# Sixteen quads and the q projection in TensorE loops, V in halves, y in two column tiles, and resident code in a decode block

## The chip, the cores and the metric

The kernel runs on one core of one Trainium2 chip. A time is the device time of one execution in microseconds (us). "Span" is the part of it that the profile covers, from the first recorded instruction to the last; a time is about 1.7 to 3.5 us longer than its span. That remainder, time minus span, is called **the closing** below. "Granted clock" is the share of TensorE's full clock that the profile lists as granted.

## The reference, cut to what matters

One decoding step for a batch of 2: layer norm of x (2 x 512), q projection, attention of 32 heads over caches of 8192 positions, output projection, residual, a second layer norm and a gated MLP.

```python
q = (layernorm(x) @ wq).reshape(2, 32, 1, 128)
scores = einsum("bhqd,bhkd->bhqk", q, k_cache) * 128 ** -0.5   # k_cache: 2 x 32 x 8192 x 128, bf16
o = einsum("bhqk,bhkd->bhqd", softmax(scores), v_cache)        # v_cache: the same size
h = x + o.reshape(2, 1, 4096) @ wo
n = layernorm(h)
gate, up = n @ W_gate, n @ W_up                                # 512 x 1376 each
out = h + (relu(gate) * up) @ W_down                           # 1376 x 512
```

The caches are 268 of the 281 MB that have to be read, and every byte is used once.

## The kernel before

K and V pass in 16 "quads" (four heads of one batch element: 8.39 MB of K, 8.39 MB of V). There are two K buffers and one V buffer. For each quad VectorE multiplies K by q and halves the row by additions, then a reduction (`sums`) gives the scores; ScalarE takes the exponentials; TensorE does 64 matmuls with V; VectorE picks the useful lanes of their result (`lanes`); and after four quads four "spread" matmuls and a `gather` bring the heads into place.

```python
def products(n, lo, hi):                       # K x q, then halving additions, all on VectorE
    s.op("dve", lambda: dve.tensor_tensor(out=kp, in0=kp, in1=..q.., op=ALU.mult), ...)
    while width > 8:
        s.op("dve", ..add the two halves of kp..)
...
def fn():                                      # TensorE: 15 quads in a loop, the 16th unrolled
    with pe.Fori(0, NGR * B) as g:
        ..four spread rows..
        with pe.Fori(0, NS - ((g + 1) >> 2)):
            pe.wait_ge(s.sem("v_in"), 16).then_inc(s.sem("v_in"), -16)
            pe.wait_ge(s.sem("p_in"), 1).then_inc(s.sem("p_in"), -1)
            pe.wait_ge(s.sem("o_in"), 1).then_inc(s.sem("o_in"), -1)
            v_matmuls(vt, o_ps[0], 0, T).then_inc(s.sem("pe"), 1)
...
for n in range(L):                             # L = 15
    scores(n, ...)                             # products, sums, exps
    if n + 2 < N: load_k(n + 2)
    if n % NS == 1 and n > 1: gather(n // NS - 1)
    if n: lanes(n - 1)
    if n + 1 < L: load_v(n + 1)
```

The last quad is unrolled: V15 goes into K14's buffer in three pieces and wo into the V buffer in four. All bulk loads are issued by SyncE on one queue, in one fixed order. wq comes first, then K0 in two halves, K1, V0 and so on to W_down. x and the last row of x are small loads issued by ScalarE.

At the end of the program each engine's instructions are laid out in blocks: a `head`, a branch round the looping part, a `rest`, a branch hint to `done`, and a spare block of one nop.

The softmax here doesn't subtract the row's maximum and nothing guards it: scores larger than these inputs give would overflow.

## Time and profile before

| | before |
|---|---|
| time, median of 3 (range) | 660.89 us (659.88 to 661.23) |
| span of the profiled run, whose time was 661.17 | 658.0 us |
| busy share: VectorE, ScalarE, TensorE | 94%, 9%, 18% |
| read | 281.06 MB at 427 GB/s |

Two groups of the page, beside what the prediction shows. The columns are line, engine, operation, operands, count, then busy us and mean ns of one, then the idle time just before the group and what ended most of it.

```profile
L383 DVE TENSOR_TENSOR k<-k,qrep 128x32768 bf16<-128x32768 bf16 (+3 forms) x18 | 275.9, 15327 | 3.6 <-DMA k<-in_A_k_cache_dram 3.6
L365 ACT ACTIVATE qrep<-mm 32x512 bf16<-32x512 f32 x12 | 7.1, 588 | 2.4 <-PE mm L352 2.1
```

In the whole execution VectorE waits 3.6 us for K. The timeline of the start and of the end (start, busy us, engine, line, operation, wait in brackets):

```profile
1.53 2.52 ACTq L290 DMA_DIRECT2D osb<-in_A_x_dram  x1
...
10.37 0.29 PE L313 MATMUL st<-ident,osb 2*128 2x2 bf16 x4 [10.37 <-DMA osb<-in_A_x_dram]
...
14.90 3.63 PE L352 MATMUL mm<-v,om 128*64 128x512 bf16 x16 [1.97 <-DMA v<-in_A_wq_dram]
...
21.68 0.33 SPq L283 DMA_DIRECT2D v<-in_A_v_cache_dram  x1
```
```profile
654.73 0.29 DVE L745 CAST sc<-y 128x128 bf16<-128x128 f32 x1 [1.90 <-PE y L674]
655.04 0.64 SPq L748 DMA_DIRECT2D out_dram<-sc  x1
```

### The profile page before, as it was taken

The page shows a single profiled execution, that of the slowest core. Times are in us where ns is not written, and L with a number is a line of the kernel's source. Part 1 is how long each engine was busy: PE and PEld are TensorE (multiplying, and loading weights), DVE is VectorE, ACT ScalarE, POOL GpSimd, SP SyncE. Part 2 cuts the span into 40 slices and gives each one's busy share as a digit, 9 for nine tenths or more (in the row PEclk, how much of TensorE's full clock was granted, in tenths as well). Part 3 has the DMA queues.
Part 4 walks back from the last instruction along what each step waited for, and adds up shares of the span by engine and source line. Part 5 has one row for each costly group of instructions (what it writes and reads, how often), then busy time and mean ns, then how long its engine had stood idle before and what let it go on. Part 6 is the DMA issues. An engine that isn't in the chain of part 4 may idle for free.

```text
span 658.0 us, 3127 instructions
## 1 busy us (share of the span) xinstructions
PE 116.6 (18%) x1240; PEld 47.6 (7%) x1240; DVE 617.8 (94%) x182; ACT 59.5 (9%) x155; POOL 6.5 (1%) x28
## 2 busy tenths in 40 slices
PE   1300301103030110303002030300303030030365
PEld 1100100001010000101001010100101010010122
DVE  1699999999999999999999999999999999999973
ACT  1401001010101001010100101010010101001110
POOL 3000000000000000000000000000000000000000
PEclk9755655756565575655557565565756556575656
DMA  9999999999999999999999999999999999999996
GB/s 377 450 442 430 406 442 446 442 430 406 442 446 442 430 406 442 446 442 430 406 442 446 442 430 406 442 446 442 430 406 442 446 442 430 406 442 446 412 410 267
DMA packets 6763, 281.09 MB, mean 427 GB/s; under 512 B 772, under 2 KB 872, under 8 KB 1640
## 3 DMA queue, kind: packets, MB, share of 16 engines
q1 hardware_dynamic: 6744, 281.06, 99.0%
q8 instruction: 1, 0.02, 0.0%
q14 instruction: 2, 0.02, 0.0%
q10 hardware_dynamic: 16, 0.01, 0.0%
HBM read 281.06 MB, written 0.00 MB: 427 GB/s over the span
## 4 chain that ended last, share of the span: by engine, by line
DVE 80%; DMA 19%; issue 1%; SPq 0%; PE 0%
DVE k L383 37%; DVE k L389 36%; DMA k<-in_A_k_cache_dram 16%; DVE sc L238 5%; DMA k<-in_B_W_down_dram 3%; DVE osb L472 1%; DVE om L468 1%; SPq L548 0%; SPq L560 0%; DVE ou L238 0%; DVE rep L484 0%; SPq L292 0%; PE y L674 0%; DVE sc L745 0%; SPq L821 0%
## 5 line engine op out<-in xcount | busy, mean ns | idle before, releaser
L383 DVE TENSOR_TENSOR k<-k,qrep 128x32768 bf16<-128x32768 bf16 (+3 forms) x18 | 275.9, 15327 | 3.6 <-DMA k<-in_A_k_cache_dram 3.6
L389 DVE TENSOR_TENSOR k<-k 128x4096 bf16<-128x4096 bf16 (+6 forms) x72 | 267.4, 3714 | 2.5
L425 PE MATMUL o<-v,pm 128*32 128x512 bf16 x960 | 86.5, 539 | 461.6 <-PEq L452 461.6
L402 ACT ACTIVATE pm<-sc 32x256 bf16<-32x256 f32 (+2 forms) x68 | 48.2, 709 | 561.6 <-DVE sc L238 560.9
L425 PEld LDWEIGHTS o<-v,pm 128*32 128x32 bf16 x960 | 36.2, 130 | 511.8 <-issue 506.1
L238 DVE TENSOR_REDUCE sc<-k 128x256 f32<-128x2048 bf16 (+2 forms) x17 | 36.7, 2160 | 0.6
L472 DVE TENSOR_REDUCE osb<-om 128x128 f32<-128x512 f32 x16 | 16.5, 1028 | 0.6
L402 ACT ACTIVATION_READ_ACCUMULATOR pm<-sc 32x1 f32 x68 | 15.9, 233 | 0.0
L432 PE MATMUL rep<-osb,spread 128*32 128x128 f32 x40 | 3.9, 420 | 50.0 <-DVE osb L472 47.1
L468 DVE TENSOR_TENSOR om<-o,turn_of 128x512 f32<-128x512 f32 x16 | 10.9, 681 | 1.8 <-PE o L425 1.8
L320 DVE COPY xc<-st 128x8 f32<-128x8 f32 x1 | 0.2, 167 | 10.7 <-PE st L313 10.7
L425 PE MATMUL o<-k,pm 128*32 128x512 bf16 x64 | 7.4, 629 | 7.3 <-ACT pm L402 4.6
L368 DVE CAST qrep<-mm 32x512 bf16<-32x512 f32 x4 | 2.8, 696 | 5.1 <-PE mm L352 5.1
L365 ACT ACTIVATE qrep<-mm 32x512 bf16<-32x512 f32 x12 | 7.1, 588 | 2.4 <-PE mm L352 2.1
L352 PE MATMUL mm<-v,om 128*64 128x512 bf16 x32 | 6.3, 546 | 2.4 <-DMA v<-in_A_wq_dram 2.0
L541 POOL TENSOR_TENSOR zm<-zm,zx 128x1 f32<-128x1 f32 x1 | 0.2, 189 | 619.2 <-ACT pm L402 619.2
L640 DVE STREAM_TRANSPOSE osb<-mm 128x512 f32<-128x512 f32 x1 | 0.7, 717 | 5.1 <-PE mm L624 5.1
L432 PEld LDWEIGHTS rep<-osb,spread 128*32 128x32 f32 x40 | 1.4, 146 | 52.5 <-DVE osb L472 48.7
L624 PE MATMUL mm<-v 128*2 128x512 bf16 x32 | 4.1, 609 | 0.9 <-DMA v<-in_A_wo_dram 0.8
L425 PEld LDWEIGHTS o<-k,pm 128*32 128x32 bf16 x64 | 2.0, 134 | 12.3 <-ACT pm L402 6.0
L352 PEld LDWEIGHTS mm<-v,om 128*64 128x64 bf16 x32 | 2.5, 149 | 5.8 <-DVE pick L238 2.0
L313 PE MATMUL st<-ident,osb 2*128 2x2 bf16 x4 | 0.3, 172 | 10.4 <-DMA osb<-in_A_x_dram 10.4
(86 smaller groups left out, 35.1 us busy)
## 6 DMA issues: line engine op xcount, KB each, us to landing
k<-in_A_k_cache_dram SPq DMA_DIRECT2D x2, 4096.0 KB, 27.7
v<-in_A_wq_dram SPq DMA_DIRECT2D x1, 4096.0 KB, 13.8
k<-in_A_v_cache_dram SPq DMA_DIRECT2D x1, 4096.0 KB, 31.4
k<-in_A_v_cache_dram SPq DMA_DIRECT2D x1, 3072.0 KB, 38.3
v<-in_A_wo_dram SPq DMA_DIRECT2D x1, 2048.0 KB, 17.6
k<-in_B_W_gate_dram SPq DMA_DIRECT2D x1, 1376.0 KB, 14.7
k<-in_B_W_up_dram SPq DMA_DIRECT2D x1, 1032.0 KB, 16.8
k<-in_A_v_cache_dram SPq DMA_DIRECT2D x1, 1024.0 KB, 40.3
```

The costliest lines, as they stand in the source:

```text
L238: s.op("dve", lambda: dve.tensor_reduce(out=out_, in_=in_, axis=axis, op=ALU.add), reads=reads, writes=writes)
L352: last = pe.matmul(out=ps[h * B * Q:(h + 1) * B * Q], lhsT=xnb[:, c].rearrange("p b q -> p (b q)"), rhs=wq_h[:, c, g:g + QP, h0 + h, :], s ...
L365: s.op("act", lambda src=src, dst=dst: act.activation(out=dst, in_=src, func=ACT.Copy), reads=[f"mm{t}"], writes=[key])
L368: s.op("dve", lambda src=src, dst=dst: dve.tensor_copy(dst, src), reads=[f"mm{t}"], writes=[key])
L383: s.op("dve", lambda: dve.tensor_tensor(out=kp, in0=kp, in1=_view(qrep[:, b, i, :], 0, [[0, hi - lo], [1, Dh]]), op=ALU.mult), reads=keys ...
L389: s.op("dve", lambda half=half, width=width: dve.tensor_tensor(out=kp[:, :, 0:half], in0=kp[:, :, 0:half], in1=kp[:, :, half:width], op=AL ...
L402: last = act.activation(out=p_of[ps, lo // TG:hi // TG, :, h], in_=sc2[n % 2][ps, lo:hi].rearrange("p (g t) -> p g t", t=TG), func=ACT.Exp ...
L425: last = pe.matmul(out=o[g:g + W2], lhsT=pm[:, t // TG, :], rhs=vs[:, t:t + TG, :].rearrange("p t d -> p (t d)"), start=(t < P // Q * TG), ...
L432: return pe.matmul(out=rep_ps[u * Q:(u + 1) * Q, :], lhsT=spread.rearrange("k h m -> k (h m)"), rhs=osb[:, u, :], start=True, stop=True, s ...
L468: s.op("dve", lambda: dve.tensor_tensor(out=om.rearrange("p (t d) -> p t d", d=Dh), in0=o.rearrange("p (t d) -> p t d", d=Dh), in1=_view(t ...
L472: fn = lambda: dve.tensor_reduce(out=osb[:, u, :], in_=om.rearrange("p (t d) -> p d t", d=Dh), axis=AXIS.X, op=ALU.add)
L624: last = pe.matmul(out=ar_ps[g:g + B], lhsT=oc[:, k, :], rhs=wo_sb[:, k, :], start=False, stop=(k + P // Q >= NK), skip_group_check=True)
```

## The change

The intent: put all looping work of TensorE into loops, so that each engine's code is one block with a small late block behind it. The code is then meant to stay resident, with fewer instruction fetches during the run and between runs. The last quad and the q projection need another shape for that.

```diff
+    SPARE = {"act": 15, "dve": 1, "pe": 7}
 ...                                          # q projection: a loop of 8 turns of 4 matmuls
-        def fn():
-            for h in range(2):
-                for c in range(KC):
-                    last = pe.matmul(out=ps[h * B * Q:(h + 1) * B * Q], ..)
+    def q_loop():
+        with pe.Fori(0, NR2 // 2) as r:
+            for t in range(2):
+                pe.wait_ge(s.sem(f"q{t}"), 1).then_inc(s.sem(f"q{t}"), -1)
+                for c in range(KC):
+                    last = pe.matmul(out=mm_ps[t][0:B * Q], .., rhs=wq_r[:, c, :, bass.ds(r * 2 + t, 1), :], ..)
+                last.then_inc(s.sem("pe"), 1)
 ...                                          # all 16 copies of q on ScalarE (before 12, and 4 on VectorE)
-                with pe.Fori(0, NS - ((g + 1) >> 2)):
-                    ..wait v_in, p_in, o_in..
-                    v_matmuls(vt, o_ps[0], 0, T).then_inc(s.sem("pe"), 1)
+                with pe.Fori(0, NS):          # all 16 quads
+                    take("v_in", 16)
+                    take("p_in", 1)
+                    take("o_in", 1)
+                    v_matmuls(0, T // 2).then_inc(s.sem("half"), 1)
+                    take("v_two", 16)
+                    v_matmuls(T // 2, LATE)
+                    take("p_two", 1)
+                    v_matmuls(LATE, T).then_inc(s.sem("pe"), 1)
 ...
-    for n in range(L):
+    for n in range(N):
 ..products(n)..
+        if n: lanes(n - 1)                    # now ahead of sums(n)
+        if n % NS == 1 and n > 1: gather(n // NS - 1)
         sums(n, 0, T, f"sc{n % 2}")
 ..exps(n), load_k(n + 2)..
-        if n % NS == 1 and n > 1: gather(n // NS - 1)
-        if n: lanes(n - 1)
-        if n + 1 < L: load_v(n + 1)
+        if n + 1 < NLOOP - 1: load_v(n + 1)
+        else:                                 # V14 and V15
+            s.last["va"] = ("half", n + 1)
+            load_v(n + 1, 0, T // 2)
+            load_v(n + 1, T // 2, T)
 ...                                          # wo: into K14's buffer, 3 pieces (before V's buffer, 4)
-        for c in range(KC):                   # y: four column tiles of 128
-            end = pe.matmul(out=y_ps[c * Q:c * Q + m], lhsT=lhsT, rhs=rhs[:, c * P:(c + 1) * P], ..)
+        for c in range(2):                    # y: two of 256
+            end = pe.matmul(out=y_ps[c * 2 * Q:c * 2 * Q + m], lhsT=lhsT, rhs=rhs[:, c * D // 2:(c + 1) * D // 2], ..)
 ...
+        if key == "wdd":                      # ahead of the last two y matmuls
+            for eng in ("pe", "dve", "act"): s.cut(eng)
-    s.op("dve", lambda: dve.tensor_copy(y_row, y_ps), ..)
+    s.op("dve", lambda: dve.tensor_copy(y_row[y0], y_ps[y0]), ..)
+    s.op("act", lambda: act.activation(out=y_row[y1], in_=y_ps[y1], func=ACT.Copy), ..)
 ...                                          # code layout of ScalarE, VectorE and TensorE
-    ..head, main, foot (branches back once), rest, hint to done, spare of one nop..
+        nc.switch_body(f"{name}_all", parent=inner, valid_engines=only)
+        loc = engine.mark_branch_hint_location()
+        s.emit(name, engine, 0, s.cuts[name])
+        engine.br_lt(turn, 9, on_true=f"{name}_late", on_false=f"{name}_spare").branch_hint(loc)
+        nc.switch_body(f"{name}_late", parent=top, valid_engines=only)
+        loc = engine.mark_branch_hint_location()
+        s.emit(name, engine, s.cuts[name])
+        engine.br_lt(turn, 9, on_true="done", on_false=f"{name}_spare").branch_hint(loc)
+        nc.switch_body(f"{name}_spare", parent=top, valid_engines=only)
+        for _ in range(SPARE[name]):
+            engine.nop("spare")
```

Cut here are the lines of the diff that move buffers and those that remove `row_of`, the memset of `osb` and the unrolled last quad.

## The prediction

> **What bounds the kernel now.** I read the page first: engines, slices, queues. Then the windows of the last microseconds, the DMA queue's own waits, and the timeline of both ends.
>
> ```profile
> PE 116.6 (18%) x1240; PEld 47.6 (7%) x1240; DVE 617.8 (94%) x182; ACT 59.5 (9%) x155; POOL 6.5 (1%) x28
> ...
> DMA  9999999999999999999999999999999999999996
> ...
> q1 hardware_dynamic: 6744, 281.06, 99.0%
> q8 instruction: 1, 0.02, 0.0%
> q14 instruction: 2, 0.02, 0.0%
> ...
> HBM read 281.06 MB, written 0.00 MB: 427 GB/s over the span
> ...
> k<-in_A_k_cache_dram SPq DMA_DIRECT2D x15, 37.3
> v<-in_A_v_cache_dram SPq DMA_DIRECT2D x15, 32.5
> ```
>
> VectorE is 94% busy and the chain of work names it for 80% of the span, which tempts one to call it the bound. But the data queue holds the 16 DMA engines for 99.0% of the span, and the 281.06 MB are the inputs, each read once. A quad is 2 x 8.39 = 16.78 MB of K and V, 39.3 us at the mean 427 GB/s; VectorE needs 17.22 + 8.69 + 4.43 + 2.29 + 1.22 + 2.29 + 0.68 + 1.03 = 37.85 us for it (mean durations by shape). So the DMA is the slower of the two. VectorE starts late, when the first half of K0 lands, and catches up by about 1 us a quad until it waits for K at the end.
>
> The last two lines give the queue's depth: a K load (8.39 MB, 19.6 us at 427 GB/s) lands 37.3 us after issue, a V load 32.5 us. So each is issued with 13 to 18 us of older transfers still ahead of it. Only what happens before the first transfer, after the last, or an issue later than this backlog can move the end.
>
> ```profile
> 24.51 8.69 DVE L383 TENSOR_TENSOR k<-k,qrep 128x16384 bf16<-128x16384 bf16 x1 [2.12 <-DMA k<-in_A_k_cache_dram]
> ...
> 595.40 12.96 DVE L383 TENSOR_TENSOR k<-k,qrep 128x24576 bf16<-128x24576 bf16 x1 [0.73 <-DMA k<-in_A_k_cache_dram]
> ...
> 636.19 0.69 DVE L468 TENSOR_TENSOR om<-o,turn_of 128x512 f32<-128x512 f32 x1 [1.79 <-PE o L425]
> ...
> 644.20 0.60 PE L624 MATMUL mm<-v 128*2 128x512 bf16 x4 [0.67 <-DMA v<-in_A_wo_dram]
> ...
> 647.61 1.44 PE L683 MATMUL o<-k,sc 128*32 128x344 bf16 x16 [1.15 <-DMA k<-in_B_W_gate_dram]
> ...
> 654.33 0.34 PE L674 MATMUL y<-k,v 128*2 128x128 bf16 x12 [0.31 <-DMA k<-in_B_W_down_dram]
> ```
> ```profile
> 651.00:652.00 1.00, 0.46 (x10) 0.07 (x6) 0.64 (x3) 0.00 (x0) 0.00 (x0) 0.87 0.97 356
> 652.00:653.00 1.00, 0.72 (x21) 0.42 (x21) 0.50 (x2) 0.18 (x1) 0.00 (x0) 1.00 0.19 57
> 653.00:654.00 1.00, 0.38 (x16) 0.21 (x16) 0.00 (x0) 0.00 (x0) 0.00 (x0) 1.00 0.07 27
> ```
>
> In the timeline (start, busy us, engine, line, operation, wait in brackets) quad 15's products wait for K15, the wo rows for wo, the gate matmuls for W_gate, the last y matmuls for W_down: to the end the work follows landings. The windows' last two columns show the stream running to 652 us. What follows, 654.7 to 658.0, is the y copy (0.29 us), the output store and the closing.
>
> [...] the bytes are given, so the middle has no slack to sell. [...] the SP queue waits 326.8 us for TensorE before V loads while the DMA engines stay 99% busy. [...] Here the instruction queues moved three packets in the whole span, 0.04 MB, all at its start, so there is no stall in the stream for resident code to remove. [...] The windows show 0.50 in the tail until 651 us, so I use the slow durations there.
>
> **The change, part by part.**
>
> q projection in a loop: 8 turns of 4 matmuls replace 4 blocks of 8, and all 16 copies of 0.588 us go to ScalarE (12 there and 4 on VectorE before). wq still lets it start at about 14.9 us. The turns now write the same 64 partitions, so I do not count on two matmuls side by side: a group costs 4 x 0.43 = 1.7 us (the trace shows two weight loads each 0.43 us where two groups ran together). Quad 0 needs the first four turns and the last of their copies: 14.9 + 4 x 1.75 + 0.6 = 22.5 us. K0's first half lands at 24.5, so about 2 us remain and VectorE starts as before. The V0 load waits for turn 8, some 29 us instead of 21.7; wq, K0 and K1 (20.97 MB, 49 us) are queued ahead of it, so that is hidden.
>
> Order on VectorE: the two `lanes` operations of quad n-1 (0.68 + 1.03 = 1.7 us) move ahead of quad n's `sums`. K(n+2) and V(n+1) are thus issued 1.7 us later, against 13 to 18 us of backlog: nothing. Work before quad 15 is the same.
>
> V14 and V15 in halves through the one V buffer; wo goes into K14's buffer. Bytes and their order (K15, V14, V15, wo, gate, up, down) stay. V15's first half is issued when V14's first half has been used, about 605 + 3.5 = 608.5 us, with V14's second half still running to 615; its second half at about 618, with the first running to 624.6. About 6 us of room each.
>
> Quad 15, the tail: VectorE does lanes(14) before its sums, so the last products, sums and the release of K15's buffer end 1.7 us later, 634.5 instead of 632.75. The gate load goes out then, about 10 us before the wo rows have landed: hidden. V15's second half lands at 634.3. Before, three pieces let 16 matmuls run at 631.8; now all 32 of the half wait for it: 634.3 + 3.6 (32 matmuls took 3.60 us at 625.48) = 638.0 instead of 636.1. So +1.9 us up to lanes(15). From there: lanes 1.75, four spread rows 0.66, gather 0.6, and the sum of z behind the spread (0.6, beside the gather), then its inverse 0.6 and the two products 0.45: 642.2. Before, wo's products began at 639.3 and were fed by landings to 644.8. Now the rows mostly lie ready: 0.5 for x and 32 x 0.107 = 3.4 put the end at 646.2, +1.4 us. The transpose-to-`hd` chain (2.0 us) ends 648.25; gate, held until 647.6 by its landing, starts +0.65. The y rows of h are two tiles of 256 columns in place of four of 128: per pass twice the columns, 0.65 becomes about 1.05, +0.4. Up then ends near 652.6 instead of 651.45, and the activation chain (2.2 us) reaches y about 653.7. Before, y waited for W_down until 654.33. Now 22 matmuls of 256 columns, the column work of the 44 of 128, need about 1.2 us and a branch inside them 0.1 to 0.2: end at 655.0 to 655.2 instead of 654.67, **+0.3 to +0.5 us**. The y copy of 2x256 is about 0.1 us longer on each of VectorE and ScalarE, side by side. Removed: `row_of`, the osb memset and the wait for its reader, 4 casts: off the path. Two output runs per row instead of four: perhaps -0.1.
>
> Sum: +0.3 to +0.6 us on 660.89. Against it stands what this profile hardly shows, the roughly 3 us between span and measured time, where resident code might give back a few tenths. I take +0.3: **661.2 us**.
>
> **The rivals.**
> First, a new wait inside the stream: an SP issue that comes when the queue has run dry. For it: one V buffer, and one issue order in which V15 holds up wo. Against it: at least 6 us of room at the worst place. If TensorE's 32 matmuls took twice as long there, it would still hold; a miss would cost its overrun, 1 to 4 us (to 665).
> Second, VectorE becomes the bound. For it: it waited only about 1.5 us for K in the last quads, so a late q projection beyond 24.5 + 1.5 would pass straight to the end. Against it: about 2 us of margin at the start. [...]
> Third, an instruction stall: the new cut branches to a late block just ahead of the last two y matmuls, on the path. [...] If the change removes a fetch between launches instead, 659.5 to 660.
> Fourth, the tail is hidden wholly[...]: 660.7.
>
> **Range and chances.** Three runs of before spread over 1.35 us. The likely course gives 660.7 to 661.5; rivals on the slow side reach 663 to 664, on the fast side 659.5. I take 659.8 to 662.9. Two per cent is 13.2 us: faster would need fewer bytes or a faster stream, slower a stall larger than any named. So 0.01, 0.975, 0.015.
>
> **What the profile of the changed kernel would show.** The data queue still near 99% and 281.06 MB at about 427 GB/s. The first product of quad 0 near 24.5, waiting for K0, right; if it waits for the copies of q, wrong. Quad 15's product still waiting for K15 near 595.4. The last V matmuls near 638, lanes(15) after them, wo's products ending near 646 and not on a landing. The last y matmul 0.3 to 0.5 us later. Wrong would be: a hole in the DMA row before 650; a fetch in the instruction queues near the end; the stream's own rate moving by over 0.3%, which nothing in the change reaches.

The sum is whole: 653.7 for the start of the last y matmuls, 1.2 us for them and 0.1 to 0.2 for the branch inside them against 654.67 before, then the copy and the output, came to +0.3 to +0.6 us, of which +0.3 was taken. "Only what happens before the first transfer, after the last, or an issue later than this backlog can move the end" was inference; run 3 moves the end by 4.2 us otherwise.

## More of the kernel before

The issue of x on ScalarE takes 2.52 us, and x is used at 10.37. At the other end the copy of y starts at 654.73, the store is issued at 655.04, and the span closes three microseconds later.

## The result and the profile after

The changed kernel took 659.87 us (median of 4 runs, 659.72 to 660.27); the kernel before, in the same rounds, took 660.78 (4 runs, 659.88 to 661.23). The ratio is 0.9989 with a 95% interval of 0.9972 to 1.0006. A ratio is the mean time of one kernel's fast runs over that of the other's of the same rounds, so it is not quite the ratio of the medians. With five more rounds later (below) the two medians were 659.87 after and 659.99 before: nothing in the typical run, but the kernel before has a tail of slower runs.

The page of the changed kernel, engines and queues:

```profile
PE 121.5 (18%) x1206; PEld 49.6 (8%) x1206; DVE 613.6 (93%) x177; ACT 61.9 (9%) x160; POOL 5.6 (1%) x25
...
q1 hardware_dynamic: 6596, 281.06, 99.0%
q8 instruction: 2, 0.03, 0.0%
q14 instruction: 4, 0.03, 0.0%
...
L386 DVE TENSOR_TENSOR k<-k,qrep 128x32768 bf16<-128x32768 bf16 (+3 forms) x18 | 275.8, 15323 | 5.9 <-DMA k<-in_A_k_cache_dram 5.9
```

Bytes, data-queue share and rate (427 GB/s) are those of before. The span (657.9 here) hardly differs. Yet the wait of VectorE for K has grown from 3.6 to 5.9 us: VectorE starts earlier and has more slack, as the timeline shows at both ends:

```profile
1.07 0.56 ACTq L292 DMA_DIRECT2D osb<-in_A_x_dram  x1
...
5.64 0.29 PE L315 MATMUL st<-ident,osb 2*128 2x2 bf16 x4 [5.64 <-DMA osb<-in_A_x_dram]
...
13.82 4.50 PE L350 MATMUL mm<-v,om 128*64 x12 [5.60 <-PEq L348]
...
20.40 0.38 DVE L243 TENSOR_REDUCE pick<-ident 128x8 f32<-128x128 bf16 x1 [10.90 <-ACT qrep L367]
...
22.94 8.69 DVE L386 TENSOR_TENSOR k<-k,qrep 128x16384 bf16<-128x16384 bf16 x1 [2.16 <-DMA k<-in_A_k_cache_dram]
...
25.02 0.33 SPq L287 DMA_DIRECT2D v<-in_A_v_cache_dram  x1
```
```profile
594.32 12.96 DVE L386 TENSOR_TENSOR k<-k,qrep 128x24576 bf16<-128x24576 bf16 x1 [0.86 <-DMA k<-in_A_k_cache_dram]
...
636.93 0.69 DVE L463 TENSOR_TENSOR om<-o,turn_of 128x512 f32<-128x512 f32 x1 [3.75 <-PE o L418]
...
641.41 3.56 PE L587 MATMUL mm<-k 128*2 128x512 bf16 x32
...
647.04 1.44 PE L645 MATMUL gate<-k,sc 128*32 128x344 bf16 x16 [0.61 <-DVE xd L625]
...
653.13 1.25 PE L635 MATMUL y<-k 128*2 128x256 bf16 x14 [0.27 <-DMA k<-in_B_W_down_dram]
...
654.42 0.41 DVE L711 CAST sc<-y 2x256 bf16<-2x256 f32 x1 [1.89 <-PE y L635]
...
654.88 0.62 SPq L716 DMA_DIRECT2D out_dram<-sc  x1
```

Three things are to be seen. K0's first half, whose load is second in the queue in both kernels, ends VectorE's wait at 22.94 instead of 24.51, and K15 at 594.32 instead of 595.40, although the stream moves the same bytes at the same rate. The wo products now run in one piece (32 matmuls, no landing in between), as predicted, and gate no longer waits for its own load. And the end is still a landing: the y matmuls wait for W_down.

### Where the landings moved

The first point contradicts the prediction. The trace records 16 completions for each load, at different times; I take each for the share of one of the 16 DMA engines that the page counts. VectorE's first product starts 0.02 to 0.03 us after the last of the 16 (before at 24.51 after 24.48, in the changed kernel at 22.94 after 22.92), so a landing counts from its last completion. Here are the completions of three loads in us (first engine to last engine), and the bytes moved by a given moment, worked out from the trace's packets (one under way counts in part):

```
                    wq               K0, first half    end of V15
before              12.69 to 14.77   22.40 to 24.48    632.13 to 634.24
after               12.71 to 13.22   22.42 to 22.92    632.16 to 633.14
MB by 200 us        before 85.40, after 85.42
MB by 650 us        before 280.18, after 280.20
```

The first engine finishes K0's half at 22.4 in both kernels. The last one is 2.08 us behind it before, 0.49 after. I call this the **spread** of a landing. Before, the last but one is 1.19 behind and the other fourteen lie within 0.51, so two engines are late there. The records do not name the engine: that it is the same one from load to load is inferred from the steady gap. The spread is the same in load after load, until something changes it:

```
spread of the next load after      12 us   50 us   100 us   300 us   590 us   640 us
before                              2.08    2.08     2.08     2.09     2.09     2.09
after                               0.51    0.49     0.49     0.98     1.00     1.01
instruction fetches, before: 8 KB at 2.35 and 4.07, 16 KB at 4.19
instruction fetches, after:  8 KB at 138.1 and 140.7, 16 KB at 642.4
```

So the working theory (**A**), which runs 3 to 5, 11 and 12 test, is this: fetches of instructions use the same 16 DMA engines as the data. The engine that carries one falls behind, and as all 16 have a share in every load (16 completions) and the queue never runs dry (99.0% of the span), it stays behind. A landing waits for the latest engine. The change moved the fetches from the first 5 us to later.

Rivals: (**B**) it is the place of x's load, which is issued earlier and quicker now; (**C**) what the change gains lies outside the span, in the closing; (**D**) the spread is chance that varies from run to run. For the end, a list of suspects: the wide y tiles, the branch to the late block, the split copy, the closing.

### The profile page after: what moved, and what is told of

Same layout as the page of the kernel before. It is cut to its first block, busy times and chain, and to the rows that moved or that the text cites. A ratio compares the mean times of both kernels' runs of the same rounds, so it can differ in the third digit from the quotient of the medians.

```text
span 657.9 us, 3103 instructions
## 1 busy us (share of the span) xinstructions
PE 121.5 (18%) x1206; PEld 49.6 (8%) x1206; DVE 613.6 (93%) x177; ACT 61.9 (9%) x160; POOL 5.6 (1%) x25
## 3 DMA queue, kind: packets, MB, share of 16 engines
q1 hardware_dynamic: 6596, 281.06, 99.0%
HBM read 281.06 MB, written 0.00 MB: 427 GB/s over the span
## 4 chain that ended last, share of the span: by engine, by line
DVE 75%; DMA 24%; issue 0%; SPq 0%; PE 0%
DVE k L386 34%; DVE k L392 33%; DMA k<-in_A_k_cache_dram 21%; DVE sc L243 4%; DMA k<-in_B_W_down_dram 3%; DVE osb L468 2%; DVE om L463 1%; SPq L539 0%; PE y L635 0%; DVE ou L243 0%; DVE rep L475 0%; SPq L551 0%; DVE sc L711 0%; SPq L294 0%; SPq L779 0%
## 5 line engine op out<-in xcount | busy, mean ns | idle before, releaser
L418 PE MATMUL o<-v,pm 128*32 128x512 bf16 x1024 | 96.3, 556 | 477.6 <-PEq L433 477.6
L418 PEld LDWEIGHTS o<-v,pm 128*32 128x32 bf16 x1024 | 39.1, 132 | 534.3 <-issue 529.5
L350 PE MATMUL mm<-v,om 128*64 x32 | 9.6, 436 | 7.1 <-PEq L348 7.0
L367 ACT ACTIVATE qrep<-mm 32x512 bf16<-32x512 f32 x16 | 9.4, 587 | 6.7 <-PE mm L350 6.5
L350 PEld LDWEIGHTS mm<-v,om 128*64 128x64 bf16 x32 | 3.9, 122 | 12.4 <-issue 11.6
L587 PE MATMUL mm<-k 128*2 128x512 bf16 x32 | 3.6, 624 | 0.0
L635 PE MATMUL y<-k 128*2 128x256 bf16 x22 | 1.8, 271 | 0.4 <-DMA k<-in_B_W_down_dram 0.3
```

What stands on the lines that cost most here:

```text
L350: last = pe.matmul(out=mm_ps[t][0:B * Q], lhsT=xnb[:, c].rearrange("p b q -> p (b q)"), rhs=wq_r[:, c, :, bass.ds(r * 2 + t, 1), :], start ...
L367: fn = lambda src=src, dst=dst: act.activation(out=dst, in_=src, func=ACT.Copy)
L418: last = pe.matmul(out=o_ps[g:g + W2], lhsT=pm[:, t // TG, :], rhs=vt[:, t:t + TG, :].rearrange("p t d -> p (t d)"), start=(t < P // Q * T ...
L587: last = pe.matmul(out=ar_ps[g:g + B], lhsT=oc[:, k, :], rhs=wo_sb[:, k, :], start=False, stop=(k + P // Q >= NK), skip_group_check=True)
L635: end = pe.matmul(out=y_ps[c * 2 * Q:c * 2 * Q + m], lhsT=lhsT, rhs=rhs[:, c * D // 2:(c + 1) * D // 2], start=first, stop=last, skip_grou ...
```

## The experiments

Runs of one call share a chip and the runs of the kernel before. The first call had runs 1 to 4 (chip 5), the second 5 to 8 (chip 4), the third 9 to 12 (chip 6). All were correct and timed in 5 rounds (run 7 in 3).

**Run 1, the kernel before, unchanged.**

> The kernel before once more, for the spans of its single runs. Theory A (code fetches take one of the 16 data engines and make every later landing late): the sixteen completions of one K load spread over about 2.1 us from the first load to the last, as in the first profile. Theory C (the gain lies outside the span, in the closing code): measured time minus span is about 3.2 us in every run, against 1.8 us in all four runs of the changed kernel. If the difference is not stable, C falls.

Measured: 659.81 us (659.43 to 661.15), spread 1.72 us until 71 us, then falling to 1.36 by 187 us and 1.3 at the end, VectorE's first product at 24.07. The nine shared runs of before spread from 659.49 to 661.16, at spans of 657.6 to 658.1. The variation of the time is not in the span: the closing goes from 1.76 to 3.46 us. The spread also differs between two executions of the same kernel, and here it drifts down by 0.4 us with no gap in the queue, so D holds in part; but it does not come near the 0.5 of the changed kernel. C in the form that was expected, 3.2 us in every run, falls.

**Run 2, the changed kernel.**

> The changed kernel once more. Theory A: spread of one load's completions 0.5 us until about 138 us, 1.0 until 642, 1.6 at the end, and K0's first half lands 1.5 us earlier than in the kernel before. Theory C: time minus span 1.8 us; span the same as or up to 0.6 us longer than before's; time 0.5 to 1.4 us under before's.

Measured: 659.87 us (659.68 to 660.11), ratio 0.9997 (0.9983 to 1.0011). Mean span 658.04 against 657.77 of the 14 runs of before on this chip: +0.27. Closing 1.78 to 1.91, against a mean of 2.31 before. Spread 0.72, then 1.34 after its fetches at 138.2 and 141.1. The change lost 0.27 us inside the span and won 0.45 in the mean of the closing, so in the mean C is right: what it gained lies outside the span. The sum of the two is within the noise of the ratio.

**Run 3, the changed kernel with 1024 nops on GpSimd**, which has nothing else to do at that time:

```diff
     build_masks()
+    def idle_code():
+        for _ in range(1024):
+            pool.nop("spare")
+    s.lists["pool"].append(((), idle_code, None))
```

> The changed kernel with 1024 idle instructions (64 KB of code) put into GpSimd's stream behind its set-up, off every path (GpSimd next has work at 637 us). Theory A: some four more code fetches of about 1.1 us show in the instruction queues before 100 us; if they fall on one data engine the spread of completions grows by up to 4 us and the time by up to 4 us; if on different ones, by about 1 us. Rival B (the lag comes from the place of the load of x, not from code): no change, within 0.2 us, spread as in the changed kernel.

Measured: 664.14 us (663.82 to 664.22), ratio 1.006, mean span 662.28. The lines of its page:

```profile
q14 instruction: 12, 0.10, 0.0%
...
HBM read 281.06 MB, written 0.00 MB: 424 GB/s over the span
...
L392 DVE TENSOR_TENSOR k<-k,qrep 128x32768 bf16<-128x32768 bf16 (+3 forms) x18 | 275.8, 15325 | 10.0 <-DMA k<-in_A_k_cache_dram 9.8
```

The nops delay nobody: no other engine waits for GpSimd there. But eight fetches of 8 KB appear between 15.1 and 53.5 us, about 5.5 us apart, VectorE's wait for K rises from 5.9 to 9.8 us, and the span by 4.2. The spread grows with the fetches and keeps what it has up to 613 us. It shrinks with V15's two halves, to 4.68 and 3.92: the first could be issued only at 612.4, because the landing of V14's first half was late, and in 610 to 615 us the DMA share is 78%. That the late engine makes up a part while the others wait there is a reading of these numbers:

```
spread after:  12.6 us 0.58   22.3 us 1.76   32.1 us 3.05   51.4 us 5.71   then 5.7 to 613 us   641.7 us 3.92
K0, second half, last engines: 32.56 and 35.10; K1: 51.93 and 57.07 (all other engines done by 51.93)
```

By these completions one engine carries all eight: (5.71 - 0.58) / 8 = 0.64 us for each 8 KB, where the packet itself took 0.31. **Theory A is right**: added code alone brings the lag. B is not needed for it, as x's load is where the changed kernel has it.

**Run 4, the changed streams in the old code layout** (the layout part of the diff undone, no cut).

> The changed kernel with the block layout and branch hints of the kernel before (one hint per engine, no cut before the last y matmuls, head block, aligned), all else as changed. Theory A and C: the code fetches of the first 5 us come back, spread near 2 us, time minus span back to 3.2 us, time 661 or more: the layout is the part that counts. If instead the loops and halves carry the gain, it stays at 659.9 with time minus span 1.8.

Measured: 659.96 us (659.75 to 660.07), span 658.08, closing 1.75 to 1.97. The early fetches are back (8 KB at 1.96 and 4.14), the spread is 1.22 from the first load, VectorE starts at 23.68, and x's issue takes 2.58 us again. So the layout moves the fetches and the early landings, as A says, but by less than expected: the early 16 KB fetch of before did not come back (it lies at 642.8, as in the changed kernel), the spread is 1.22 and not near 2, and the time is not 661 or more. The long closing that was expected to return did not either: those parts of the expectation were wrong.

**Run 5, the streams of before in the new code layout**, with the cut ahead of the last y matmuls.

> The kernel before with only the block layout and hints of the changed kernel. If the layout is what shortens the closing, time minus span is 1.8 us in all five runs (the kernel before: 1.8 to 3.5, mean 2.3) with the span at 657.6 to 657.9 as before, so 659.4 to 659.7. If the streams themselves do it (fewer instructions on TensorE and VectorE), time minus span still scatters to 3 us.

Measured: 660.12 us (659.88 to 660.29), span 658.22 (before on this chip 657.82), closing 1.79 to 1.93. A clean single case: the spread is 0.35 until one fetch of 16 KB at 77.8 us, then 1.7 to the end, **+1.4 us for 16 KB**. Two more fetches of 8 KB, at 177.1 and 198.7, bring the last completion but one from 0.35 to 1.27 us behind the first, and leave the spread as it is: by these completions they fell on an engine that was not the latest. VectorE starts at 22.78. The span loses 0.4 although the stream's early landings are better: the loss is in the tail. The closing is short here too. So either half of the change, the streams or the layout, seems to cure the scatter of the closing. That is not shown: five runs stand for each half, and of the nine runs of before on this chip five were short as well, so that five short ones in a row would come by chance in one case of twenty ((5/9)^5 = 5%).

**Run 6, the changed kernel with y in four tiles of 128** and one copy on VectorE (the y part of the diff undone).

> The changed kernel with y back in four column tiles of 128 columns, one copy by VectorE. If the two wide tiles and their copies are what lengthened the tail, the span falls from 658.04 to 657.7 or 657.8; if the order around quad 15 is the cause, it stays at 658.0.

Measured: 662.42 us (662.17 to 662.43), span 660.52, 2.5 us more: the expectation was wrong. Up to the store the wide y tiles cost little: from W_down's last landing to the store it takes 0.81 us here (0.82 in run 10) and 0.98 in run 2, which is 0.17 more with the wide tiles. The lines of this run, and of run 2 behind them, by the timeline:

```profile
655.05 0.65 SPq L716 DMA_DIRECT2D out_dram<-sc  x1
```
```profile
655.10 0.61 SPq L716 DMA_DIRECT2D out_dram<-sc  x1
```

The difference comes after. The trace's last instructions show ScalarE starting its last branch at 656.52 and its next instruction, in the `done` block, at 659.91, with all other engines waiting for it: 3.39 us. In run 2 the same step takes 0.49 us. A fetch of 8 KB is recorded at 660.5, and only one in place of two near 138. ScalarE's code is different here (no y copy in its late block). The wait is measured; its cause is not shown. The recorded fetches do not explain it: the one at 660.5 starts when the wait is over, and the three that lie in it, from 657.1 on, have ended by 658.4.

**Run 7, the changed kernel with V14 and V15 whole.**

```diff
-            s.last["va"] = ("half", n + 1)
-            load_v(n + 1, 0, T // 2)
-            load_v(n + 1, T // 2, T)
+            load_v(n + 1)
```

> The changed kernel with V14 and V15 each loaded whole through the one V buffer. V15 can then be issued only when all of V14 has been used, near 620 us, while the queue has run dry near 613: a hole of about 8 us in the transfers, of which the engine that lags gets about 1 us back. Span 664.5 to 666.5. If instead the time stays at 660, the halves hide nothing and the room that the prediction counted did not matter.

Measured: 669.27 us (668.82 to 670.09; 4 runs), span 667.5 in the mean: 9.4 us over the changed kernel, more than expected. The windows of the profiled run, the slowest of the four (us, busy of each engine, clock, and in the last two columns the DMA share and GB/s) show the hole:

```profile
606.00:610.00 4.00, 0.00 (x0) 0.00 (x0) 3.97 (x2) 0.00 (x0) 0.00 (x0) 0.50 0.76 328
610.00:614.00 4.00, 0.00 (x0) 0.00 (x0) 4.00 (x1) 0.00 (x0) 0.00 (x0) 0.50 0.49 213
614.00:618.00 4.00, 3.46 (x36) 1.51 (x40) 3.93 (x3) 0.00 (x0) 0.00 (x0) 0.50 0.00 0
618.00:622.00 4.00, 2.82 (x36) 1.03 (x28) 3.57 (x4) 0.00 (x0) 0.00 (x0) 0.76 0.35 115
```
```profile
620.86 0.33 SPq L287 DMA_DIRECT2D v<-in_A_v_cache_dram  x1
...
643.13 5.64 PE L418 MATMUL o<-v,pm 128*32 128x512 bf16 x64 [22.31 <-PEq L433]
...
656.67 1.40 PE L643 MATMUL gate<-k,sc 128*32 128x344 bf16 x16 [0.45 <-DVE sc L619]
...
663.36 1.34 PE L633 MATMUL y<-k 128*2 128x256 bf16 x14 [0.46 <-DMA k<-in_B_W_down_dram]
```

With one V buffer, V15 can be issued only when V14 is used up, at 620.86; nothing else is queued by then, and DMA stands at zero. The data packets stop at 613.7 and start again at 621.8, and every later landing is some 10 us later than in the changed kernel: V15's last part 642.69 against 633.14, W_down's 664.13 against 653.86. At the end y still waits for W_down, so the 9.4 us are the hole itself, carried to the end by the landings. Halves are what make the single buffer work. The hole also serves theory A: the spread, 1.33 us at V14's landing (612.78 to 614.11), is 0.42 at V15's (642.27 to 642.69). Once the queue has run dry, the late engine has caught up.

**Run 8, the changed kernel with the old order** of `lanes` and `gather` behind `sums`.

> The changed kernel with lanes and gather behind sums again in quads 0 to 14 (K and V loads issued 1.7 us earlier); quad 15 as changed. The prediction says hidden: span 658.0, within 0.15. If the queue's depth mattered, the span falls by up to 1 us.

Measured: 660.06 us (659.63 to 660.15), span 658.14 against 658.04 of run 2 (on another chip, where the span of before is 0.05 longer): hidden, as expected.

**Run 9, the changed kernel with 13 instead of 15 filler nops on ScalarE; run 10, run 6's kernel with 17.** These ask whether the place of ScalarE's code, which the filler moves, explains run 6.

> The changed kernel with 13 instead of 15 never-executed filler instructions in ScalarE's stream, nothing else. In the run with y in four tiles ScalarE had two instructions fewer in front of the common closing block and waited 3.4 us for it after its last branch. If the place of that block in ScalarE's code is the cause, the same wait comes here: span near 660.5, time near 662.4. If the y tiles were the cause, nothing changes: 658.0 and 659.9.

> y in four column tiles again, with ScalarE's filler raised from 15 to 17 to make up for the two instructions that it lost. Place of the block: the wait goes away, span 657.8 to 658.1, time 659.7 to 659.9, and what is left of the difference to the changed kernel (658.04) is the true cost of the wide y tiles, which the prediction put at 0.1 to 0.4 us. Y tiles as the cause: stays at 660.5.

Measured: run 9 took 659.99 us (659.74 to 660.25), closing 1.75 to 1.84, no wait: the expectation was wrong. Run 10 took 662.16 (661.91 to 662.29): ScalarE again branches at 656.45 and goes on at 659.79. Two nops more or less neither make nor mend the wait. It comes with the y part of the diff, in both runs that take that back; what decides it stays open.

**Runs 11 and 12, 512 and 256 nops on GpSimd**, the dose of run 3 halved twice.

> As the run with 1024 idle instructions on GpSimd, with 512 (32 KB). There 64 KB made one data engine late by 5.1 us, 0.64 us per 8 KB, and the time longer by 4.2. The landing waits for the latest engine only, so 32 KB make that engine late by 0.6 + 2.6 = 3.2 us against the 2.0 of the changed kernel's latest: time +1.2 us, 660.9 to 661.5. If every fetch simply adds to the time: +2.1, 662.0.

> The same with 256 (16 KB): that engine is late by 0.6 + 1.3 = 1.9 us, no later than another engine already is at the end. If only the latest engine counts, the time stays at 659.9, within 0.2; if every fetch adds to the time, 660.9.

Measured: run 11 took 661.07 us (660.82 to 661.12), span 659.18; run 12 took 659.98 (659.87 to 660.05), span 658.10, no more than the changed kernel's own. Both as expected. The spread shows why it isn't simple adding:

```
                12 us   22 us   32 us   109 us   590 us   640 us    span
256 nops         0.39    1.69    1.69     1.68     1.66     1.70    658.10
512 nops         0.64    1.65    2.96     2.96     2.96     2.97    659.18
1024 nops        0.58    1.76    3.05     5.72     5.72     3.92    662.28
```

Two fetches early put one engine at 1.69; at the end, where the changed kernel's own latest engine stands at 1.6 to 2.0 after its fetch at 642, that is covered. **Only the latest engine counts.**

### The end, put together

From the last landing of W_down to the start of the last instruction, 0.05 us before the end of the span, profiled runs, us (worked out from the trace):

```
                                 last landing    to the copy of y    copy to store    store to last   sum
before and run 1 (mean)             654.17             0.345             0.32            2.86        3.52
after and runs 2, 8, 9 (mean)       653.99             0.52              0.46            2.99        3.97
run 4: wide y, no cut               654.21             0.48             0.46            2.83        3.77
run 5: four tiles, cut              654.07             0.55              0.32            3.02        3.89
```

The tail became 0.45 us longer: 0.18 for the last y matmuls (the wide tiles alone or the cut alone make most of that, run 4 and run 5), 0.14 because the copy of 2x256 takes 0.41 us where the one of 128x128 took 0.29, and 0.13 behind the store, where GpSimd has one more branch to close (missing in run 4, present in run 5; in the first two profiles it takes GpSimd 0.31 us from clearing its semaphores to its closing nop with that branch, and 0.12 without). The last landing came 0.18 us earlier in the mean. 0.45 - 0.18 = 0.27, the measured difference of the spans. With the profiles of before at 654.38 and 653.96, the 0.18 is no firmer than the scatter of single executions.

### The closing

Time minus span. The kernel before: 32 runs on three chips, 1.76 to 3.46 us, 14 of them at 1.97 or less. The changed kernel and all its variants (with run 5): 58 runs, 1.74 to 1.97 throughout. Of the two profiled runs of before, the one with a closing of 3.2 us recorded a fetch of 16 KB at 660.26, after the span; the one with 2.1 recorded none there. In the changed kernel the last fetches lie at 656.9 to 657.4, inside the span, beside the output store. That suggests that before sometimes fetches code after its end. Two profiles are too few to call it shown.

No version tried beats both kernels: the fastest of the others is within 0.2 us of the changed kernel. The pieces could be combined (the closing of the new layout without its cut, y in four tiles), but run 6 shows that taking y back alone costs 2.5 us at the end of the span.

## Why the prediction was right or wrong

The class and the range were right; the time was 1.3 us too high, by the median of its runs. The range held by luck: 659.87 lies 0.07 us above its lower end and below the "likely course" of 660.7 to 661.5. No rise of the time was seen; the difference to the kernel before is within the noise. Point by point:

- **Bound, bytes, rate: right.** 281.06 MB at 427 GB/s, 99.0% in both. That the middle "has no slack to sell" held. (39.3 less 37.85 is 1.45 us a quad, not "about 1".)
- **"The stream's own rate moving by over 0.3%, which nothing in the change reaches": the rate is right, the inference from it to landings was wrong.** This is the step that failed: the page's three packets in the instruction queues were read as "no stall in the stream for resident code to remove". But behind those three packets (32 KB; the 0.04 MB adds up rounded numbers) the last of the 16 completions stands 2.08 us behind the first at every landing of the execution, against 0.5 in the changed kernel: 1.6 us. Run 3 shows the cause, runs 11 and 12 the size. "No stall" is doubtful too: the issue of x takes 2.5 to 2.8 us where a fetch of 8 KB starts beside it at 2.0 to 2.4 (before, runs 1 and 4), and 0.56 without one (after, run 5). It was hidden behind wq. The prediction therefore had VectorE starting at 24.5 (measured 22.94 and 22.99) and quad 15 near 595.4 (594.32). It cost the total little, as the end of the stream depends on the latest engine there, and a fetch at 642 puts that back to 1.6 to 2.0. One of the prediction's own signs of being wrong thus came true: "a fetch in the instruction queues near the end", at 642.4 and three from 656.9 on.
- **q projection in a loop: hidden, right; its size was too pessimistic.** The last copy for quad 0 was put at 22.5; pick, which waits for the copies of q, starts at 20.40. A turn of four matmuls takes about 1.7 us in the first two, as assumed, but 1.05 from the third, at 17.3, on. That no two run side by side held: before, two matmuls went in each 0.43 us at first (16 in 3.63) and in 0.27 at the end (8 in 1.06), here one does. The profile lists the granted clock as 1.00 throughout, so what made the first two slow is not shown. V0 was issued at 25.0, not 29, and was hidden, as said.
- **Order on VectorE: hidden, right** (run 8, 0.1 us).
- **Halves: right.** The room, put at 6 us, was about 5: V15's halves went out at 607.8 and 617.5, the first engine ended what was ahead of them at 612.7 and 622.5, and there is no hole in the DMA row. Run 7 shows that the halves were needed, and that the rival of a dry queue, put at 1 to 4 us for halves, costs 9.4 when V is whole.
- **Tail of quad 15: mechanism right, 1.1 to 1.2 us too late.** The last V matmuls were predicted to end at 638.0 and ended about 636.9; the wo rows 646.2 against 644.97; gate 648.25 against 647.04. wo's rows feed in one piece as said. The error is the landing of V15's last part, 633.14 where the prediction took 634.3 from before's trace.
- **y: the bound was named wrongly.** The prediction had y released by the activation chain, about 653.7, and no longer by W_down. (Its 653.7 does not follow from the 2.2 us that it names, as 652.6 + 2.2 is 654.8; in before's timeline 1.1 us lie between the end of up, 651.4, and the first y matmul, 652.55.) As the chain came earlier, W_down's landing still ends the wait (0.27 and 0.44 us). Of the single terms, the h rows took 1.02 us (put at 1.05, 0.65 before) and the branch 0.18 from its start at 653.83 to the next instruction (put at 0.1 to 0.2). The 22 matmuls took more than the 1.2 and the branch: 0.60 + 1.25 = 1.85 us with the branch and the gaps about it (the 44 before took 0.40 + 0.39 + 0.34 = 1.13). So the sum of +0.3 to +0.6 came close to the span's +0.27 by luck, for another reason: the tail's own +0.45, less 0.18 of landing.
- **The copy and the closing.** "About 0.1 us longer" for the copy: measured 0.12. "Perhaps -0.1" for two output runs a row: from the first issue to the last landing of the output 1.85 us against 1.91. "A few tenths" that resident code might give back between span and time: measured 0.45 in the mean. It was named, but the +0.3 taken was added to 660.89, the median of three runs of which two must have had long closings: 660.89 and 661.23 lie about 3 us above the span of before in every list here (657.5 to 658.2), 659.88 about 2. The changed kernel has none of these. An estimate from before's mean span, 657.8, the predicted +0.3 and the short closing, 1.85, gives about 660.0. This is most of the 1.3 us.
- **Instruction stall at the new cut: not in this kernel.** The branch there takes the 0.18 us above. Run 6 pays 2.5 us at its last branch (3.39 us against 0.49 in run 2); the cause is not shown.
- **A tail hidden wholly (the fourth rival): not seen.** The granted clock of 645 to 650 us was 0.82 against 0.50 before, but the end follows W_down's landing all the same (a wait of 0.27 us).

## What to carry to other kernels

When a queue keeps all DMA engines busy (99.0% here), ask of each landing which engine was last, not only what the mean rate is. By the completions an instruction fetch delays one engine, a fetch of 8 KB by 0.58 to 0.65 us (runs 3, 11, 12), one of 16 KB by about 1.4 (one case, run 5), and here for hundreds of microseconds (run 3, from 53 to 613; in run 1 the spread fell by 0.4). The lag was made up nearly whole only where the queue ran dry (run 7, 1.33 to 0.42 us). It costs where work waits for landings and the delayed engine is the latest (run 11, 1.1 us of span), and else nothing (run 12, 0.1). A buffer that has just enough room needs loads in halves (run 7: 9.4 us without), and a median of three runs with a 1.4 us scatter must be split into span and closing before sums of tenths are added to it. Removing a wait inside a stream that other landings bound moves slack, not the end (here VectorE's wait for K from 3.6 to 5.9 us, the span from 658.0 to 657.9).
